# A seven-product SwiGLU kernel on one Trainium2 core: batch 0's val from unscaled tokens, 1/rms along rows by DMA, and all instruction orders redealt

## The chip, the cores and the metric

The kernel runs on one core of one Trainium2 chip. The metric is device microseconds of one execution. A profile of one execution stands beside the times. The engines are called PE (TensorE, matmuls), DVE (VectorE), ACT (ScalarE), POOL (GpSimd) and SP (SyncE, which issues most DMAs).

## The reference

`x` is (8, 8, 512, 64): batch, head, token, width. `state` is (8, 8, 32, 64). Attention goes both ways, and the tokens of all heads are then put side by side and sent through a feed-forward block:

```python
a = softmax(x @ state.T / 8);     xread = a @ state     # 512 tokens per batch
a2 = softmax(state @ x.T / 8);    sread = a2 @ x        # 32 tokens per batch
t = concat([xread, sread]) as (8 * 544, 512)
n = t / sqrt(mean(t * t, -1) + 1e-6) * rms_g
out = (silu(n @ w_gate) * (n @ w_val)) @ w_out          # 512 -> 1536 -> 512
```

The four weight arrays come as 64-bit floats and the kernel turns their bit patterns into 32-bit floats itself.

## The kernel before, in words

**Stages.** The tokens of one batch are one unit of work. Batch 0 is computed while the weights are still being loaded and converted. Batches 1 to 7 follow, each with the same sequence; while PE computes the products of batch b, the attention of batch b+1 is put in between. The 256 tokens of all states come last.

**Own weights.** Since `xread = a @ state`, the hidden products need not go over the 512 wide tokens: `own_weights` (L603) multiplies each batch's states by one pair of weight blocks ("pair mp", 256 columns of gate and of val; six pairs a batch; L616) and puts the result, v, into SBUF (L628). The hidden products are then of v with `aT_s`, the softmaxed scores (256 x 512 for a batch). `aT_s` is multiplied by 1/rms beforehand (L501), so gate and val both come out normalized.

**Weights at the start.** Eighteen pieces of 1 MB of raw bits (gate, val, out for each pair) are loaded, four ahead. ACT makes the exponents (`exponents`, L240, L243, L246), DVE the values (`values`, L267, L270, L276). Converted pairs are stored to DRAM and fetched again for each later batch (`fetch`, L189) into three buffers.

**Batch 0.** `scores` transposes x on PE (L334), ACT copies it (L336), PE multiplies it by the states (L361). `tokens_read` makes the softmax on DVE and ACT (L440 to L457), transposes it on PE (L465), and ACT copies it to `aT_s` (L468). The sum of squares goes over the Gram matrix of the states (L478, L481) and matmuls with a column of ones (`rms_on_array`, L392). `hidden` (L648) makes gate and val for one block of 128 hidden units (L659), silu (L665) and product (L669). The output projection goes on as blocks get ready (`project_as_ready`, L866) and is copied out by ACT (`projected`, L883).

**Batches 1 to 7.** `hidden_seven` (L753) makes the hidden products two blocks at a time by seven products in place of eight (L763), with sums on DVE (L826, L839, L845, L851). `project_twice` (L1035) does the output projection by seven outer products "o", each of seven inner ones (L1066), with sums of quarters and halves on DVE (L1114 to L1125) and of results on DVE (L1106) and POOL (L1092 to L1097). The weights' quarters for it are made once, on POOL, in batch 1 (`weight_quarters`, L1020), stored, and fetched.

**The read of tokens in a batch.** Within batch b, `tokens_read(b + 1)` runs: scores (L361), softmax, DVE transposes into `aT_s` (L460), a matmul that makes the tokens for their rms (L487), squares on ACT (L494), sums on DVE (L497). Then batch 1 uses `rms_on_array` (four matmuls with ones, L392), later batches `rms_on_blocks`: a matmul with `groups` (L415), the addition of 1e-6 (L420) and a power on POOL (`mean_root`, L293), which leaves 1/rms as 128 x 4. `along_rows` spreads that along the rows of all partitions by four transposes on PE (L300), and L501 multiplies `aT_s` by it. `slot_sums` (L681 to L684, POOL) makes the sums that the seven products need.

**States.** `states_read` makes the softmax of the other direction, the matmul with x (L557), a scaling on DVE (L568), a transpose on PE (L572). `state_norm` (L577) makes the rms of all 256 state tokens with eight matmuls by ones (L585).

**What sets the order.** Nothing is left to a scheduler. Each stage is a set of generators, one letter each, and strings say which generator takes its next step: `ORDER` for the start and batch 0, `FIRST` for batch 1, `PERIOD` for batches 2 to 6, `LAST` for batch 7, `STATES` for the end. The order of steps in the string is the order of instructions on every engine, and of the DMAs on the queue of the engine that issues them. `z` in `ORDER` is a matmul of the identity that keeps PE busy (`keep_awake`, L1198).

```python
for stream in FIRST if b == 1 else LAST if b + 1 == B else PERIOD:
    next(streams[stream])
```

The functions that the change touches:

Of the kernel before, what the change touches and what calls it, by code (L numbers as in the profile page):

```python
# [8 lines left out]
F32 = mybir.dt.float32  # L9
# [5 lines left out]
ALU = mybir.AluOpType  # L15
# [4 lines left out]
P = 128  # L20
RAW_AHEAD = 4
W_BUFS = 3
FLAT = 1793.0

ORDER = (
    "ddzzzzzzzzzezzzeezaaaaaaaaaaaaddaezddaseaaazzaeaaazzdaaaazdeezzzazzaaaazeeaaaadd"
    "aaadaaeAdadsdeezezAdavaaAvAAAAvhehteeAeAdddduhhppdAddtdeeedvvvudeeedphhdtheeddtA"
    "ddddeupdAAAdhAdedeeuedppvpsdAvvddAedhhpetudeeeddhtsAAdhudpAeppdddeAAeedddvAdsvvA"
    "eedphhtuseessseedddeeAhtsdhesppsdvdupdvvdhheeAddAdAtsshtpAudApAedpdhededdveuAApA"
    "AAvvheAdAtSAASSeSSdphSddShAtASuShAkuSSwwpwwkcpSScpSkkckpkcwkkkkkwwwwk"  # L30
)

PERIOD = (
    "vlhhatthhtaxxhvuxuthhthuhtauuhhtuhuhuthtahtuaaahuhhtuhuhuxhxtutxhthukkkhtaakavfx"
    "xxvgahuhuthuuuxhthhuuxtahtaaaaahuaxhuthhtuhhthhthhsppusuuuuffutaauuhpsspuppppukp"
    "ukkkkckkaakkgppkkcpppakooskakakakkppppacpppappppcckpfppcakakapppaakkkasskkgkaagg"
    "pppppppppppaakakkooakgapssskaaakkkoosspppcfpaawwsslpssxxxpcoowxxxfg"
)

FIRST = (  # L40
    "vhththhhthfhhuuuhtttuqqqqaxxaaauhthhhvquuhuxqxxaavtuhhththhfaxthhhqqquuuuxxtuhut"
    "hthhthhuaakaavfuuxhtuuhutthqqfhhutxxuqqqqqqhauthuuxhhaautthaaasshtuuhuuthuGhskuk"
    "GuGukkppqqpppqpppugqqpkkkklkppqpppkcpcqgaakppgqqkskaakaaaaqqppkkpppkppkkpkpkpkpa"
    "cosaaaacgpapgaskkkkkkaosaapppppgcppppcaappaskkakkapppkpapkappaakpookkoosaassfsww"
    "xssswxlscxxcoxofxg"
)
LAST = (
    "vxhhffththhtuhhhavuttuuhhtfuhhgxxthhhuuuxxtuthuhtthuhuxhutuvxxxvhthhutkxghhtuhut"
    "kxxhuukhtuhthhthhhhhuuuuttuthhhuuuuhtuhuutuupphuukkppcpapkkkkkpppppppppppkkkpcpp"
    "ckkppkckpkkpkpckkkpppkkkpkoppkpppagcpppppfkpkkkkkkkkppaaaapkpggppppacpcggooooooo"  # L50
    "a"
)
STATES = (
    "hththtyyhuhuhhttuhhhyyytyuhutuhhhutthtuyyhhuuyhhthhhuyututyyyhhtyuhhthuuuhhuhtth"
    "ythuuuyyyutuhuhuytuuyhthhuuhthtuhuhutuuppkhpuucppkkccpkpkpc"
)
# [3 lines left out]
def kernel(  # L60
# [62 lines left out]

    def load_state(b):

        rows[b] = two.tile([P, 2, D], F32, name="rows")
        for j in range(4):
            src = state[b, 2 * j:2 * j + 2].rearrange("e n d -> n e d")
            nc.sync.dma_start(out=rows[b][Ns * j:Ns * j + Ns], in_=src)

# [35 lines left out]
    x_d = [scratch.tile([4, 4, Ns, 4 * P], F32, name="x_d%d" % k) for k in range(2)]  # L166
    e_d = [scratch.tile([4, Ns, 4, 8 * Ns], F32, name="e_d%d" % k) for k in range(2)]
    w_sb = {}
    wo = consts.tile([P, NM, DM], F32, name="wo")
# [4 lines left out]
    for mp in range(NM // 2):  # L174
        for dram in (moe_w_gate, moe_w_val):
            pieces.append(dram[:, 2 * P * mp:2 * P * mp + 2 * P].rearrange("(i p) f -> p i f", p=P))
        pieces.append(
            moe_w_out[2 * P * mp:2 * P * mp + 2 * P].rearrange("(m p) f -> p m f", p=P))
# [12 lines left out]
    def home(k):  # L191

        mp, kind = divmod(k, 3)
        if kind == 2:
            return wo[:, 2 * mp:2 * mp + 2].rearrange("p m (i f) -> p m i f", f=P)
        return (w_sb[mp] if kind else new_w(mp))[:, :, :, kind, :]

# [108 lines left out]
    def scores(b, packed, soft):  # L306
# [22 lines left out]
        if b < 2:  # L329
            xT = one.tile([P, 4, NC, P], F32, name="xT", tag="xT")  # L330
            for c in range(NC):
                tp = aps.tile([P, 4, P], F32, name="at")
                for j in range(4):
                    TE.transpose(out=tp[:, j, :], in_=xb[:, c, P * j:P * j + P], identity=ident)  # L334
                yield
                SE.copy(xT[:, :, c, :], tp)  # L336
                yield "step"
# [48 lines left out]
    def rms_on_array(b, sq):  # L386

        sp = aps.tile([P, NC], F32, name="at") if b else fy.tile([P, NC], F32, name="f")
        order = (0,) if b else (0, 1)
        for i in order:  # L390
            for c in range(NC):
                TE.matmul(out=sp[:, c:c + 1], lhsT=sq[:, i, P * c:P * c + P], rhs=ones,  # L392
                          start=(c == 0 and i == order[0]),
                          stop=(i == order[-1]), skip_group_check=True)
        yield
        ss = two.tile([P, NC], F32, name="ss")
        VE.tensor_scalar(ss, sp, 1e-6, None, op0=ALU.add)
        yield "step"
        ri = mean_root(ss, NC)
        yield  # L400
        rp = along_rows(ri, NC) if b else along_rows(ri, NC, vps, "pv")
        yield
        return rp

    def rms_on_blocks(b, sq):
# [18 lines left out]
        yield  # L424
        rp = along_rows(ri, NC)
        yield
        return rp

    def tokens_read(b):
# [21 lines left out]
        for e in range(2):  # L451
# [15 lines left out]
            yield  # L467
            SE.copy(aT_s[b][:, e], tp.rearrange("p c t -> p (c t)"))  # L468
            yield "step"
# [13 lines left out]
        else:  # L483
# [12 lines left out]
            for i, j in ((0, 1), (2, 3), (0, 2)):  # L496
                VE.tensor_tensor(out=sq[:, i, :], in0=sq[:, i, :], in1=sq[:, j, :], op=ALU.add)  # L497
                yield
        rp = yield from (rms_on_array if b < 2 else rms_on_blocks)(b, sq)
        for e in (slice(0, 2),) if b else (slice(0, 1), slice(1, 2)):  # L500
            VE.tensor_tensor(out=aT_s[b][:, e], in0=aT_s[b][:, e],  # L501
                             in1=rp.unsqueeze(1).to_broadcast([P, e.stop - e.start, S]), op=ALU.mult)
        yield "step"
# [73 lines left out]
    def state_norm():  # L577

        sq = one.tile([P, NI, NT], F32, name="sqT", tag="eS")
        SE.activation(out=sq, in_=xsT, func=ACTF.Square, scale=DM ** -0.5)  # L580
        yield
        sp = aps.tile([P, NT // P], F32, name="at")
        for r in range(NT // P):
            for i in range(NI):
                TE.matmul(out=sp[:, r:r + 1], lhsT=sq[:, i, P * r:P * r + P], rhs=ones,  # L585
                          start=(i == 0), stop=(i == NI - 1))
        yield
# [15 lines left out]
    def own_weights(b, mp):  # L603
# [4 lines left out]
        def products():  # L608
            w = w_sb.pop(b * (NM // 2) + mp)
            for e in range(2):  # L610
                pv.append(vps.tile([P, 4 * P], F32, name="pv") if b and mp % 2 == 0 else
                          aps.tile([P, 4 * P], F32, name="at") if b or mp else
                          fx.tile([P, 4 * P], F32, name="f"))
            for j in range(4):
                for e in range(2):
                    TE.matmul(out=pv[e][Ns * j:Ns * j + Ns, :],  # L616
                              lhsT=stT_g[b][D * e:D * e + D, j, :],
                              rhs=w[D * e:D * e + D, j].rearrange("p m k f -> p (m k f)"),
                              start=True, stop=True)
            if b == 0 or b == 1 and mp < 2:  # L620
                fetch(b * (NM // 2) + mp + W_BUFS)
            yield

        def copies():
            v = (seven["v"] if b else v_0).tile([P, 2, 2, 2, P], F32, name="v")
            v_sb[b, mp] = v, None
            for e in range(2):
                SE.copy(v[:, e].rearrange("p m k f -> p (m k f)"), pv[e])  # L628
                yield
# [3 lines left out]

        return products(), copies()

    def more_of_v(b, mp):
# [10 lines left out]

    def hidden(m, lhs, rhs):  # L648


        gp, vp = [], []
        t = []
        h = hb[:, m, :]

        def products():
            for k, to in enumerate((gp, vp)):
                to.append(vps.tile([P, S], F32, name="pv"))
                for i, r in enumerate(rhs):
                    TE.matmul(out=to[0], lhsT=lhs(i, k), rhs=r,  # L659
                              start=(i == 0), stop=(i == len(rhs) - 1))  # L660
                yield

        def silu():
            t.append(two.tile([P, S], F32, name="t", tag="g"))
            SE.activation(out=t[0], in_=gp[0], func=ACTF.Silu)  # L665
            yield

        def gated():
            VE.tensor_tensor(out=h, in0=t[0], in1=vp[0], op=ALU.mult)  # L669
            yield  # L670

        return products(), silu(), gated()

# [205 lines left out]
    def projected(banks, store):  # L879
        spare = seven["s"].rearrange("p (r k) f -> p r (k f)", r=3)  # L880
        for r in range(4):
            ot = spare[:, r] if r < 3 else two.tile([P, DM], F32, name="ot", tag="g")
            SE.copy(ot, banks[r])  # L883
            store(r, 0, DM, ot)
            yield
# [298 lines left out]

    def of_batch_0(part):

        for m in range(NM):
            if m not in parts_0:
                parts_0[m] = hidden(m, lambda e, k, m=m: v_sb[0, m // 2][0][:, e, m % 2, k, :],
                                    [aT_s[0][:, e, :] for e in range(2)])  # L1190
            yield from parts_0[m][part]

    def keep_awake():
# [20 lines left out]

    parts_0, banks_0 = {}, []
    halves = load_parts(0)
# [7 lines left out]
    for k in range(2, RAW_AHEAD):  # L1224
# [4 lines left out]
               "e": exponents(), "d": values(),  # L1229
               "v": (step for mp in range(NM // 2) for part in own_weights(0, mp) for step in part),  # L1230
               "h": of_batch_0(0), "t": of_batch_0(1), "u": of_batch_0(2),
               "p": project_as_ready(banks_0), "c": projected(banks_0, store_tokens(0)),
# [69 lines left out]
```

## Time and profile before

| what | us |
|---|---|
| time, median of 3 runs (lowest, highest) | 758.01 (757.89, 759.5) |
| profiled execution: span from first to last instruction | 756.2 |
| one steady batch (381.05 to 461.21, first product to first product) | 80.2 |
| batch 1 (133.15 to 220.72) | 87.6 |
| first hidden product of batch 0 (L659) starts at | 32.46 |
| last matmul ends about | 752.8 |

The page of the profile gives the profiled execution's span but no time of its own; the median of the runs is 1.8 above the span, and that is what lies around it. Busy time is the time in which an engine has an instruction under way. The chain that ended last is followed backward from the last instruction: at each step to what released it, or to the instruction before it on the same engine. The waits list how long an engine stood for another one's result. The slices of the whole span, each 18.9 us, show PE near full from the second one on:

```profile
PE   8999999999899999999999999999999999999998
```

### The profile page before, as it was taken

What the parts mean: (1) busy time and instruction counts of PE and PEld (TensorE: products, weight loads), DVE (VectorE), ACT (ScalarE), POOL (GpSimd) and SP (SyncE); (2) the same over time, 40 slices, a digit from 0 to 9 for tenths busy, and PEclk for the clock granted to TensorE, in tenths of its full rate; (3) what the DMA queues carried; (4) which work ended last, traced back from release to release, by engine and by line L of the source; (5) the groups of instructions that cost most, each with busy time, mean ns of one, the idle gap of its engine ahead of it and who ended that gap; (6) DMA issues with size and microseconds to landing.
All of it is one profiled execution on the core that took longest, in us unless ns stands there. A gap on an engine that the chain in (4) does not pass through costs nothing.

```text
span 756.2 us, 14360 instructions
## 1 busy us (share of the span) xinstructions
PE 743.2 (98%) x5618; PEld 592.0 (78%) x5618; DVE 578.7 (77%) x979; ACT 351.7 (47%) x546; POOL 294.2 (39%) x380
## 2 busy tenths in 40 slices
PE   8999999999899999999999999999999999999998
PEld 6534444778768898879877997799788987899997
DVE  3887776679957996689947994799579965787961
ACT  5998965553235523643255425543456236411220
POOL 2000003892584326532474129312842275323600
PEclk9999999999999999999999999999999999999999
DMA  9986954695576176725684377517661865132311
GB/s 281 281 299 227 314 211 151 248 294 163 201 228 240 32 291 209 281 56 198 243 284 112 135 274 253 175 69 299 215 225 27 305 204 218 51 98 114 140 56 29
DMA packets 61891, 146.17 MB, mean 193 GB/s; under 512 B 15744, under 2 KB 32640, under 8 KB 54912
## 3 DMA queue, kind: packets, MB, share of 16 engines
q1 hardware_dynamic: 48704, 125.78, 47.8%
q10 hardware_dynamic: 13120, 19.47, 8.9%
q8 instruction: 45, 0.74, 0.4%
q14 instruction: 22, 0.18, 0.1%
HBM read 116.46 MB, written 28.77 MB: 192 GB/s over the span
## 4 chain that ended last, share of the span: by engine, by line
PE 91%; DVE 5%; ACT 3%; issue 1%; POOL 0%; DVEq 0%; POOLq 0%
PE f L763 38%; PE f L1066 28%; PE pv L659 5%; PE f L866 5%; PE at L616 3%; PE pv L616 3%; PE f L929 2%; PE f L1198 2%; PE at L557 1%; PE at L361 1%; PE at L487 1%; DVE hb L1125 0%; PE at L300 0%; ACT ex L243 0%; PE at L334 0%
## 5 line engine op out<-in xcount | busy, mean ns | idle before, releaser
L763 PE MATMUL f<-aT_s,v 128*128 128x256 f32 x504 | 119.6, 382 | 0.0
L763 PEld LDWEIGHTS f<-aT_s,v 128*128 128x128 f32 x504 | 94.5, 190 | 24.8 <-issue 8.4
L1092 POOL TENSOR_TENSOR kept<-kept 128x256 f32<-128x256 f32 x28 | 23.1, 824 | 174.9 <-DVE kept L1106 173.8
L826 DVE TENSOR_TENSOR g<-g,f 128x512 f32<-128x512 f32 x84 | 57.4, 686 | 40.0 <-PE f L763 35.9
L1076 ACT COPY kept<-f 128x512 f32<-128x512 f32 (+1 forms) x56 | 29.6, 532 | 123.9 <-PE f L1066 82.2
L763 PE MATMUL f<-aT_t,vs 128*128 128x256 f32 x336 | 87.1, 383 | 0.0
L1066 PE MATMUL f<-w,h 128*128 128x128 f32 x588 | 74.6, 276 | 0.9 <-DVE h L1116 0.8
L763 PEld LDWEIGHTS f<-aT_t,vs 128*128 128x128 f32 x336 | 62.5, 190 | 15.4 <-POOL vs L643 4.2
L1066 PEld LDWEIGHTS f<-w,h 128*128 128x128 f32 x588 | 69.6, 192 | 5.3 <-issue 4.1
L817 ACT ACTIVATE hb<-g 128x1024 f32<-128x1024 f32 x42 | 44.4, 1058 | 56.9 <-DVE g L826 56.8
L643 POOL TENSOR_TENSOR vs<-v 128x256 f32<-128x256 f32 x42 | 31.4, 748 | 79.5 <-ACT v L628 79.5
L293 POOL TENSOR_TENSOR ri<-ss,mhalf 128x4 f32<-128x4 f32 x8 | 10.7, 1341 | 116.7 <-DMA w_m<-w_d 84.1
L815 ACT COPY g<-f 128x512 f32<-128x512 f32 x42 | 24.6, 586 | 45.0 <-PE f L763 45.0
L763 PE MATMUL f<-aT_t,v 128*128 128x256 f32 x168 | 43.5, 381 | 1.6 <-DVE c L826 1.6
L866 PE MATMUL f<-wo,hb 128*128 128x512 f32 x96 | 44.8, 603 | 0.0
L659 PE MATMUL pv<-aT_s,v 128*128 128x512 f32 x96 | 43.9, 595 | 0.0
L763 PE MATMUL f<-aT_s,vs 128*128 128x256 f32 x168 | 43.6, 382 | 0.0
L839 DVE TENSOR_TENSOR hb<-hb,c 128x512 f32<-128x512 f32 (+1 forms) x48 | 36.6, 763 | 7.9 <-ACT hb L817 7.2
L839 DVE TENSOR_TENSOR hb<-hb,f 128x512 f32<-128x512 f32 (+1 forms) x48 | 31.0, 646 | 15.1 <-PE f L763 15.1
L1066 PE MATMUL f<-wo,h 128*128 128x128 f32 x336 | 42.2, 275 | 0.0
L1066 PE MATMUL f<-wo,hb 128*128 128x128 f32 x336 | 42.1, 275 | 0.0
L826 DVE TENSOR_TENSOR c<-c,f 128x512 f32<-128x512 f32 (+1 forms) x48 | 31.2, 651 | 12.6 <-PE f L763 12.6
(204 smaller groups left out, 1657.7 us busy)
## 6 DMA issues: line engine op xcount, KB each, us to landing
w_m<-w_d SPq DMA_DIRECT2D x48, 1024.0 KB, 5.8
w<-t_d SPq DMA_DIRECT2D x49, 576.0 KB, 5.1
out_dram<-kept SPq DMA_DIRECT2D x56, 128.0 KB, 1.9
raw<-in_moe_w_val_dram SPq DMA_DIRECT2D x6, 1024.0 KB, 5.4
raw<-in_moe_w_out_dram SPq DMA_DIRECT2D x6, 1024.0 KB, 8.5
w_d<-w_m SPq DMA_DIRECT2D x6, 1024.0 KB, 4.9
x_b<-in_x_dram SPq DMA_DIRECT2D x6, 1024.0 KB, 7.7
x_d<-xB ACTq DMA_DIRECT2D x6, 1024.0 KB, 4.2
```

Of the source, the lines that this page charges most:

```text
L616: TE.matmul(out=pv[e][Ns * j:Ns * j + Ns, :], lhsT=stT_g[b][D * e:D * e + D, j, :], rhs=w[D * e:D * e + D, j].rearrange("p m k f -> p (m k ...
L643: GE.tensor_tensor(out=vs[:, 0], in0=a21, in1=a22, op=ALU.add)
L659: TE.matmul(out=to[0], lhsT=lhs(i, k), rhs=r, start=(i == 0), stop=(i == len(rhs) - 1))
L763: TE.matmul(out=ps[:, i, 0:half], lhsT=l[:, i, :], rhs=r, start=(start and i == 0 and k == 0), stop=(k == len(lhs) - 1), skip_group_check= ...
L815: SE.copy(gates(q)[1], q["x"][:, :, 0:half])
L817: SE.activation(out=hb[:, 2 * mp:2 * mp + 2, 0:n].rearrange("p m (c t) -> p m c t", c=2), in_=q["g"][:, :, :, 0:half], func=ACTF.Silu if s ...
L826: VE.tensor_tensor(out=to, in0=to, in1=q[ps][:, :, 0:half], op=ALU.add)
L839: VE.tensor_tensor(out=part, in0=part, in1=val, op=ALU.mult)
L866: TE.matmul(out=banks[r], lhsT=hb[:, m, P * r:P * r + P], rhs=wo[:, m, :], start=(m == 0), stop=(m == NM - 1))
L1066: TE.matmul(out=to[half][:, slot, :], lhsT=lhs[:, k, :], rhs=rhs[:, k, :], start=(fresh and n in (0, 4) and k == 0), stop=(k == QM - 1), s ...
L1076: SE.copy(k[:, 4 * i:4 * i + 4 - i], banks[name][i])
L1092: GE.tensor_tensor(out=k[:, 1:3], in0=k[:, 0:1].to_broadcast([P, 2, QD]), in1=k[:, 1:3], op=ALU.add)
```

## The change

- **Orders.** All five strings are dealt anew.
- **Pieces.** The val piece of a pair is loaded and converted ahead of its gate piece.
- **Batch 0, tokens.** `aT_s` is kept unscaled. The row of 1/rms is copied to SBUF (`row`) and a scaled copy `aT_n` is made. Val products use `aT_s`. Gate products use `aT_s` for the first two blocks, whose result is multiplied by `row`, and `aT_n` for the rest. Since val is left without its 1/rms, `projected` multiplies each row of tokens by it (a column of `ri`).
- **Batch 0, pair 0.** `first_own_weights` makes val's half and then gate's half of the own weights.
- **Copies.** Copies of xT alternate between ACT and DVE; one of batch 0's two `aT_s` copies, and one of each two v copies, goes to DVE.
- **1/rms along rows.** From batch 1 on, `rms_on_blocks` is used, and 1/rms goes to DRAM and comes back broadcast to all partitions, by two DMAs on SP, in place of the four transposes.
- **Banks.** For batches 2 to 7, the own weights of pair 1 go to the banks `fy` and `fz`.
- **state_norm.** The four squares are added on DVE, and two matmuls with ones are left of eight.

The strings apart, the core of the diff is:

```diff
-        for dram in (moe_w_gate, moe_w_val):
+        for dram in (moe_w_val, moe_w_gate):
...
-                SE.copy(xT[:, :, c, :], tp)
+                (VE.tensor_copy if c % 2 else SE.copy)(xT[:, :, c, :], tp)
...
         ri = mean_root(ss, NC)
         yield
-        rp = along_rows(ri, NC)
-        yield
-        return rp
+        nc.sync.dma_start(out=r_d[b % 2].rearrange("c p -> p c"), in_=ri)
+        yield
+        nc.sync.dma_start(out=sq[:, 2, :], in_=r_d[b % 2].rearrange("c p -> (c p)")
+                          .unsqueeze(0).to_broadcast([P, S]))
+        yield
+        return sq[:, 2, :]
...
-            SE.copy(aT_s[b][:, e], tp.rearrange("p c t -> p (c t)"))
+            (VE.tensor_copy if e else SE.copy)(aT_s[b][:, e], tp.rearrange("p c t -> p (c t)"))
...
-        rp = yield from (rms_on_array if b < 2 else rms_on_blocks)(b, sq)
+        rp = yield from (rms_on_blocks if b else rms_on_array)(b, sq)
+        to = aT_s[b]
+        if b == 0:
+            row = rms_0["row"] = x_0.tile([P, S], F32, name="row")
+            SE.copy(row, rp)
+            rp = row
+            yield
+            to = x_0.tile([P, 2, S], F32, name="aT_n")
+            aT_n.append(to)
+        VE.tensor_tensor(out=to, in0=aT_s[b], in1=rp.unsqueeze(1).to_broadcast([P, 2, S]),
+                         op=ALU.mult)
...
+        for n in (NI // 2, NI // 4):
+            VE.tensor_tensor(out=sq[:, 0:n], in0=sq[:, 0:n], in1=sq[:, n:2 * n], op=ALU.add)
+            yield
         sp = aps.tile([P, NT // P], F32, name="at")
         for r in range(NT // P):
-            for i in range(NI):
-                TE.matmul(out=sp[:, r:r + 1], lhsT=sq[:, i, P * r:P * r + P], rhs=ones,
-                          start=(i == 0), stop=(i == NI - 1))
+            TE.matmul(out=sp[:, r:r + 1], lhsT=sq[:, 0, P * r:P * r + P], rhs=ones,
+                      start=True, stop=True)
...
+    def first_own_weights():
+        w = w_sb[0]
+        v = v_0.tile([P, 2, 2, 2, P], F32, name="v")
+        v_sb[0, 0] = v, None
+        for k in (1, 0):
+            pv = [fx.tile([P, 2, P], F32, name="f") for e in range(2)]
+            for j in range(4):
+                for e in range(2):
+                    TE.matmul(out=pv[e][Ns * j:Ns * j + Ns],
+                              lhsT=stT_g[0][D * e:D * e + D, j, :],
+                              rhs=w[D * e:D * e + D, j, :, k, :], start=True, stop=True)
...
+            for e in range(2):
+                (VE.tensor_copy if e else SE.copy)(v[:, e, :, k, :], pv[e])
+                yield
...
+        def product(pool, name, m, k, tokens):
+            ps = pool.tile([P, S], F32, name=name)
+            for e in range(2):
+                TE.matmul(out=ps, lhsT=v_sb[0, m // 2][0][:, e, m % 2, k, :], rhs=tokens[:, e],
+                          start=(e == 0), stop=(e == 1))
+            return ps
...
+            for m in range(2):
+                v[m] = product(vps, "pv", m, 1, aT_s[0])
+                yield
+            for m in range(2):
+                g[m] = product(fx, "f", m, 0, aT_s[0])
+                yield
+            for m in range(2, NM):
+                g[m] = product(vps, "pv", m, 0, aT_n[0])
+                yield
+                v[m] = product(vps, "pv", m, 1, aT_s[0])
+                yield
...
+            for m in range(2):
+                VE.tensor_tensor(out=new_t(m), in0=g[m], in1=rms_0["row"], op=ALU.mult)
+                yield
...
-            SE.copy(ot, banks[r])
+            SE.mul(ot, banks[r], rms_0["column"][:, r:r + 1])
```

## The prediction, made before the changed kernel was run

> **What bounds the kernel.** I read the clock first, then busy time, then the chain that ended last, then a table by stage, then what TensorE (PE) waits for. The granted clock is 1.00 all through, so no step is about it.
>
> ```profile
> PE 743.2 (98%) x5618; PEld 592.0 (78%) x5618; DVE 578.7 (77%) x979; ACT 351.7 (47%) x546; POOL 294.2 (39%) x380
> PE 91%; DVE 5%; ACT 3%; issue 1%; POOL 0%; DVEq 0%; POOLq 0%
> ```
>
> PE is busy nearly always and is 91% of the chain: what PE does is what the span costs, so an instruction taken from PE is paid out in full where PE waits for nobody. Where it does wait shows by stage (columns: window, then PE, PEld, DVE, ACT, POOL busy with counts, clock, DMA share, GB/s):
>
> ```profile
> 133.00:221.00 88.00, 83.75 (x672) 68.52 (x665) 72.01 (x118) 33.57 (x58) 60.74 (x66) 1.00 0.68 222
> 381.00:461.00 80.00, 80.00 (x670) 68.19 (x662) 64.57 (x115) 34.97 (x59) 34.73 (x45) 1.00 0.59 199
> ```
>
> The lower row is a steady batch (batches 2 to 6): PE is busy 80.00 of 80.00. The upper row is batch 1, which runs from 133.15 to 220.72, 87.6 against 80.2 for a steady one (381.05 to 461.21). In the first batch-1 window PE waits for VectorE (DVE):
>
> ```profile
> PE f L763 <- DVE c L826: 1.6, 1, 1.6
> PE at L487 <- DVE aT_s L460: 1.0, 1, 1.0
> PE f L1066 <- DVE h L1116: 0.8, 1, 0.8
> PE at L572 <- DVE sr L568: 0.7, 1, 0.7
> ```
>
> So three places have something to win or lose: PE's own work everywhere, the start, and batch 1; and the steady batch, which has no wait, can only get one. These are the rows I price with (start, duration, engine, line, tile):
>
> ```profile
> 452.28 0.13 PE at L415 x2
> 455.19 0.44 PE at L300 x4
> 664.91 1.68 PE at L585 x16
> 423.83 0.68 DVE L839 TENSOR_TENSOR hb<-hb,f 128x512 f32<-128x512 f32 x1
> 441.57 0.70 DVE L460 STREAM_TRANSPOSE aT_s<-eS 128x512 f32<-128x512 f32 x1
> 442.93 0.66 PE L487 MATMUL at<-aT_s,rows 32*64 32x512 f32 x4
> 453.20 1.39 POOL L293 TENSOR_TENSOR ri<-ss,mhalf 128x4 f32<-128x4 f32 x1 [1.54 <-DVE ss L420]
> out_dram<-kept SPq DMA_DIRECT2D x56, 128.0 KB, 1.9
> rms_g<-in_moe_rms_g_dram SPq DMA_DIRECT2D x1, 2.0 KB, 7.2
> ```
>
> **1. PE work that goes: -4.9.** The four transposes that spread 1/rms along rows (L300) take 0.44 in the chain. They go in batches 1 to 7: 28 transposes at 0.44 / 4 = 0.11, 3.1. Batch 1's sum of squares goes from four ones-matmuls (0.81, from 112.81 to 113.62) to the groups matmul of the later batches (0.13): 0.7, and I take 0.6. state_norm's eight ones-matmuls (1.68 for 16 records) become two: 1.68 x 6/8 = 1.26. Sum 4.9. It is on the path because PE is; the two DVE adds that replace the six matmuls (0.69 and about 0.4) lie beside PE's projection, and the pow and the spread behind them have at most 0.5 of PE wait to give, which I put into the end's bounds.
>
> **2. The start: +0.8.** Batch 0's first hidden product starts at 32.46, and before it PE mostly waits. The change wants the val product earlier, from tokens not yet scaled. By the new order of instructions it does not get it. (a) Seventeen keep-awake matmuls stand ahead of the first transpose instead of thirteen; 4 are 8 records at 0.21, 1.7, so the step at 9.33 comes at about 11.0. (b) ACT's second xT copy now stands behind two exponent steps of 0.73; the scores matmul, at 13.36, comes at about 15.2. (c) From about 17.1 DVE has its instructions back to back up to the copy of v: reading the old rows for each, some 16 us, to 33.1. The work it got there (two xT copies 1.1, one aT_s copy 0.6, v's copy 0.35, small ones 0.5) is more than what left it (L501, 1.28). With one more xT copy (0.55) and the scaling of the state read (0.45) the first val product comes at 34.5, 2.0 later. (d) But by then PE has done more of what it must do anyway: e transposes 0.86, the state read 1.03, one chunk of x 0.43, and 0.43 of row transposes stand later; 1.9 in all. Net 0.1. (e) Then pair 1's own weights wait about 0.5 and the first gated block about 0.25 for conversions on DVE (43.5 against 42.95): +0.75. Pair 2 is converted at 58.1 for a need at 58.65, pair 3 at 71.8 for 76.9, so nothing is added there. Bounds: if DVE's queue does not hold, the tokens are ready at 25.2 and PE starts at about 27, -5.4; if (d) is wholly lost to waits, +2.5.
>
> Where the new gate work hides: in batch 0 m = 0 and 1 need one more DVE multiply each (0.69), m from 2 on read the scaled copy. The last copies (L883) become a multiply by a column on ACT; I take the 0.6 of ACT's other copies of 128x512 for it, and ACT is busy 47%.
>
> **3. Batch 1: -4.5.** Its excess is 7.4. DVE is busy 72.0 against 64.6, since its operations are stretched while GpSimd does the weight quarters (L1020): L845 takes 1.37 at 161.61, 0.68 in a steady batch. In the new order 23 of the 28 quarter steps stand ahead of the first projection step (17 before), the tokens of batch 2 arrive at its scores some 27.4 us into the batch instead of 33.4, and the DVE work that PE waited for after the hidden part is done before it. One wait stays: the read of tokens (now L490) stands after three of the seven outer products instead of four, and DVE is no faster there. I leave 2.5 to 3 of the 7.4. Bounds: all of it goes, -7.4; none, 0.
>
> **4. Steady batches: 5 x 0.8 = +4.0.** This is what the DMA costs in place of the transposes, by way of the order. To make time for a trip to DRAM and back, the read of tokens moves from 442.93 to where, in the old trace, PE stands at 437.5. It needs DVE's second aT_s transpose, which ends at 441.57 + 0.70 = 442.27, 0.66 ahead of its reader. In the new order I count the DVE instructions from the last gate product (L839 at 423.83) to that transpose: 13.8 to 14.5 us by their old rows, so it ends at 437.9 to 438.5. PE then waits 0.4 to 1.0, and about 0.2 more for the quarter sum behind it. I take 0.8. Bounds: 0 if DVE is only 0.5 faster than I count; 1.3 each, 6.5, if the projection's sums wait as well.
>
> The DMA itself: two transfers in a row, ri (128x4) to r_d as 512 separate elements, and r_d back, broadcast to 128 partitions of 2 KB. They were not in the old kernel. The groups matmul stands 13.2 us ahead of the next batch's first product in the new order; ri is ready 2.9 later (DVE 0.33 and 0.67, pow 1.39, hand-overs), and L511's multiply takes 1.22, so **the pair may take 9.0 us** at no cost. The nearest rows: a 128 KB store lands in 1.9, twice that is 3.8; rms_g, the same 512 elements of 4 bytes, took 7.2 amid the first loads, twice that is 14.4. The return is 256 KB in long runs, nearer to the store, and the write is to DRAM with far fewer bytes than rms_g's neighbours in the queue; I take 6, hidden. SP issues both and stands at each until its data is there; behind them wait one store of 128 KB and the fetch of pair 3's weights (below). Behind the multiply (L511) on DVE wait the two scalings of the state read, and for those PE's transpose of it. The Trainium skill, "DMA: Bandwidth & Descriptors", Rules for kernel authors, speaks against this form: a strided last dimension becomes one descriptor per element, and the data should be laid out contiguously instead. Its section Anatomy of one DMA gives about 2.0 us fixed plus bytes over 436 GB/s, by which the pair would be an estimated 4.6; by that too it stays hidden, and only rms_g's row says otherwise. Batch 1's pair has 24.7 us.
>
> **5. Pair 3's weights: 6 x 0.2 = +1.2.** The next batch's own weights of pair 3 move up from 465.84, 4.6 after its first product, to right behind that product. Their 1 MB goes into the buffer that pair 0 gives back, so it can be issued only when PE is through with pair 0. From there PE has, by the rows of the chain, 1.02 (pair 1), 1.03 (state read), 0.67, 0.13, 0.67, 0.13, 0.86 and 1.02 (pair 2), 5.5. In the old trace these loads landed in 5.1 at the least and 5.5 in the median of three. So PE waits between nothing and 0.6; I take 0.2, for batches 2 to 7.
>
> **6. End: 0, bounds -0.5 and +0.5.** The last batch and the states are redealt, but after the last matmul (752.8) there is 3.4 of copy and store either way, and only 0.5 of wait for hb ahead of it.
>
> **Sum.** -4.9 + 0.8 - 4.5 + 4.0 + 1.2 = -3.4. From the span of 756.2 that gives 752.8. Runs have a median of 758.0, 1.8 more than the profiled span, which I add: **754.6**.
>
> **Rivals.**
> A. The start is won: if DVE reaches the first val product's inputs by 29 instead of 33, then 3.5 to 5.4 are saved there instead of 0.8 lost, and the time is about 749.5. For it: the tokens are needed without the scaling. Against it: L501's 1.28 is all that this takes from DVE ahead of it.
> B. Slower: **the DMA pair is late.** PE's first product of a batch waits for L511, and all behind it. It decides from 9.0 us a pair; in the six batches with that room, at 9.6 the gain is gone (3.4 / 6). With 11.0, from between the two rows, it is 6 x 2.0 = 12 and the time 767; with 14.4 it is 32. For it: rms_g's 7.2. Against it: the 1.9 row, and 24.7 us in batch 1.
> C. DVE is late at the read of tokens by 1.3 in every batch, and batch 1 gains only 2.5 to 4.5 for the same reason: -4.9 + 0.8 + 6.5 + 1.2 less that is -0.9 to +1.1, 757 to 759, and 760.5 with the weights 0.5 late. For it: that transpose has 0.66 to spare now and is asked 5 us sooner. Against it: the old order puts 5 us of quarter sums ahead of it that can stand behind.
> D. The change does not do what it says: val from unscaled tokens begins no sooner than before. That is already in my start term, and giving it up wholly changes nothing more.
>
> **Chances.** Forecast 0.60 (750.5 to 756.5, its own range from the bounds of batch 1 and the steady batches), A 0.09, C 0.19, B 0.12. "Same" is within 0.2%, 756.5 to 759.5, about what a measurement here can tell. Faster: the forecast and A, 0.69. C gives 0.13 same and 0.06 slower; with B slower is 0.18. Range 749 to 760.5: it leaves out B and the far end of A, some 0.15 to 0.2.
>
> **What would show it.** The first val product near 34.5 (A: by 29). In steady batches no along-rows transposes, one wait of PE on aT_s of 0.4 to 1.0 at the read, one on the weights of pair 3 of 0 to 0.6, and a period of 80.2 - 0.44 + 1.0 = 80.8 (C: 81.3 and more). The r_d transfers landing within 9.0 together; if L511 is what the first product waits for, B. Batch 1 near 83. What would make me wrong: a DMA pair above 9.0, DVE's count before the read, or DVE's queue in the start being shorter than I add up.

## The result

The changed kernel takes 845.5 us (median of 4 runs, 841.7 to 845.8) against 758.1 for the kernel before: a ratio of 1.113 (95% interval 1.110 to 1.116). The profiled execution, the fastest of the four, has a span of 839.9, 83.7 more than before. The forecast was 754.6, in a range of 749 to 760.5.

In the page of the changed kernel, busy time, granted clock and the chain show at once that it is bound by something else:

```profile
PE 756.0 (90%) x5588; PEld 602.2 (72%) x5588; DVE 581.2 (69%) x999; ACT 362.6 (43%) x549; POOL 283.1 (34%) x380
...
PEclk9999999899999987999699997999799997999999
...
PE 59%; DMA 17%; DVE 16%; POOL 3%; issue 2%; ACT 2%; ACTq 1%; DVEq 0%; POOLq 0%
```

PE's share of the chain is 59% instead of 91%, DMAs have 17% where they had none, and PE's clock is no longer full everywhere. What PE waits for (first lines of the waits; total, times, longest):

```profile
PE at L567 <- DMA e<-e_d: 63.3, 6, 12.9
PE f L1123 <- DMA w<-t_d: 3.7, 1, 3.7
```

L567 is the read of states (L557 before). Its e, the softmax numbers of the other direction, goes to DRAM and back (e_d) to be turned round. The issues of DMAs, before and after (KB each, median us to landing):

```profile
e_d<-eB ACTq DMA_DIRECT2D x6, 512.0 KB, 3.0
e<-e_d ACTq DMA_DIRECT2D x24, 128.0 KB, 3.2
```

```profile
e_d<-eB ACTq DMA_DIRECT2D x6, 512.0 KB, 9.3
e<-e_d ACTq DMA_DIRECT2D x24, 128.0 KB, 7.2
sq<-r_d SPq DMA_DIRECT2D x7, 256.0 KB, 4.6
...
r_d<-ri SPq DMA_DIRECT2D x7, 2.0 KB, 10.1
```

Nothing was changed about e's transfers themselves. One steady batch in time shows who stands beside them: the instructions before the change, those after it, and then PE, clock and DMA after it by stretches of 8 us (columns as in the prediction). DVE turns e, ACT issues the store and the loads, PE reads:

```profile
443.57 1.24 DVE L539 STREAM_TRANSPOSE eB<-e 128x1024 f32<-128x1024 f32 x1
444.84 0.35 ACTq L542 DMA_DIRECT2D e_d<-eB  x1
447.94 2.05 ACTq L546 DMA_DIRECT2D e<-e_d  x4
456.57 1.10 PE L557 MATMUL at<-x_b,e 128*32 128x64 f32 x64
```

```profile
298.62 0.38 SPq L425 DMA_DIRECT2D r_d<-ri  x1
299.63 1.23 DVE L549 STREAM_TRANSPOSE eB<-e 128x1024 f32<-128x1024 f32 x1
300.90 0.35 ACTq L552 DMA_DIRECT2D e_d<-eB  x1
308.51 0.33 SPq L427 DMA_DIRECT2D sq<-r_d  x1
310.28 2.65 ACTq L556 DMA_DIRECT2D e<-e_d  x4
313.21 1.22 DVE L511 TENSOR_TENSOR aT_s<-aT_s,sq 128x1024 f32<-128x1024 f32 x1 [9.37 <-DMA sq<-r_d]
319.24 1.07 PE L567 MATMUL at<-x_b,e 128*32 128x64 f32 x30 [12.14 <-DMA e<-e_d]
```

```profile
300.00:308.00 8.00, 7.10 (x79) 5.52 (x78) 3.84 (x6) 0.00 (x0) 4.42 (x7) 1.00 0.72 66
308.00:316.00 8.00, 0.00 (x0) 0.00 (x0) 1.47 (x3) 2.05 (x4) 1.34 (x2) 0.61 0.79 214
316.00:324.00 8.00, 4.76 (x79) 4.62 (x80) 0.77 (x3) 0.03 (x1) 4.97 (x8) 0.53 0.88 290
```

The 2 KB of 1/rms are issued at 298.62. From 300 to 308 all queues together move 66 GB/s. e's store is issued at 300.90, ACT issues the loads at 310.28, when it has landed, and they end at 319; PE has stood still for 12 us by then, and works at half its clock behind that.

Where the 83.7 come from, by the first hidden product of each batch:

| stretch | before | after | difference |
|---|---|---|---|
| up to batch 1 | 133.1 | 131.5 | -1.5 |
| batch 1 | 87.6 | 97.4 | +9.8 |
| batches 2 to 6 | 400.9 | 477.5 | +76.6 (15.3 each) |
| batch 7 and states | 134.6 | 133.5 | -1.2 |

### The profile page after: what moved, and what is told of

It is laid out like the page before. It is cut to its first block, busy times and chain, and to the rows that moved or that the text cites. A ratio compares the mean times of both kernels' runs of the same rounds, so it can differ in the third digit from the quotient of the medians.

```text
span 839.9 us, 14333 instructions
## 1 busy us (share of the span) xinstructions
PE 756.0 (90%) x5588; PEld 602.2 (72%) x5588; DVE 581.2 (69%) x999; ACT 362.6 (43%) x549; POOL 283.1 (34%) x380
## 4 chain that ended last, share of the span: by engine, by line
PE 59%; DMA 17%; DVE 16%; POOL 3%; issue 2%; ACT 2%; ACTq 1%; DVEq 0%; POOLq 0%
PE f L820 29%; PE f L1123 12%; DMA e_d<-eB 7%; DMA e<-e_d 5%; PE pv L693 4%; PE f L923 4%; PE f L986 2%; PE at L628 2%; DVE h L1171 1%; PE pv L628 1%; DMA xG<-x_d 1%; DVE sq L500 1%; PE at L567 1%; DVE kept L1163 1%; DMA w<-t_d 1%
## 5 line engine op out<-in xcount | busy, mean ns | idle before, releaser
L1149 POOL TENSOR_TENSOR kept<-kept 128x256 f32<-128x256 f32 x28 | 20.8, 743 | 166.4 <-DVE kept L1163 155.9
L641 ACT COPY v<-pv 128x512 f32<-128x512 f32 x42 | 22.7, 589 | 114.2 <-issue 97.5
L567 PE MATMUL at<-x_b,e 128*32 128x64 f32 x512 | 13.0, 278 | 63.3 <-DMA e<-e_d 63.3
L567 PEld LDWEIGHTS at<-x_b,e 128*32 128x32 f32 x512 | 11.4, 148 | 69.5 <-issue 43.0
L677 POOL TENSOR_TENSOR vs<-v 128x256 f32<-128x256 f32 x42 | 33.5, 798 | 80.5 <-ACT v L641 80.5
L511 DVE TENSOR_TENSOR aT_s<-aT_s,sq 128x1024 f32<-128x1024 f32 x7 | 8.6, 1225 | 61.5 <-DMA sq<-r_d 61.5
L896 DVE TENSOR_TENSOR hb<-hb,c 128x512 f32<-128x512 f32 (+1 forms) x48 | 33.1, 690 | 13.0 <-ACT hb L874 12.2
```

Source lines behind the costliest of these rows:

```text
L567: TE.matmul(out=rp[Ns * j:Ns * j + Ns, e, :], lhsT=(e2T[:, j, e, c, :] if b > 1 else flat[:, e, c, Ns * j:Ns * j + Ns]), rhs=(xb[:, h, c, ...
L641: (SE.copy if b or not e else VE.tensor_copy)(v[:, e].rearrange("p m k f -> p (m k f)"), pv[e])
L677: GE.tensor_tensor(out=vs[:, 0], in0=a21, in1=a22, op=ALU.add)
L896: VE.tensor_tensor(out=part, in0=part, in1=val, op=ALU.mult)
```

## The experiments

Theory 1: the write of 512 single elements holds up the DMAs around it. Rival 2: the new order has e's store too near its reader (in the traces DVE starts to turn e 13.0 us ahead of the read before the change; after it 7.5 ahead of 307.1, when PE is ready for the read). Rival 3: SP stands at the return and lets a burst go.

**Take the trip away.** rows_on_PE spreads 1/rms by PE again:

```diff
-        nc.sync.dma_start(out=r_d[b % 2].rearrange("c p -> p c"), in_=ri)
         yield
-        nc.sync.dma_start(out=sq[:, 2, :], in_=r_d[b % 2]...to_broadcast([P, S]))
-        yield
-        return sq[:, 2, :]
+        rp = along_rows(ri, NC)
+        yield
+        return rp
```

> The changed kernel with 1/rms spread by four transposes on PE again in all batches, and no trip through DRAM; everything else, the orders too, as changed. Theory 1 (the write of 512 single elements holds the DMA engines, and the store and loads of e behind it come late): the store of e lands in 3 to 3.5 us (9.3 with the write), PE's wait at the read of states falls from 12 to at most 2.5 a batch, the time to 755 to 768. Rival 2 (the new order has the store of e 7.5 us ahead of its reader where it was 13.1, and that is what PE waits for): the wait stays at 8 or more, the time above 815.

Measured: 768.3, ratio 1.014 (1.009 to 1.019). e's store lands in 2.7, and PE waits 4.8 for e in all, at most 1.3 at once:

```profile
e_d<-eB ACTq DMA_DIRECT2D x6, 512.0 KB, 2.7
```

```profile
PE at L565 <- DMA e<-e_d: 4.8, 6, 1.3
```

The time is at the upper end of theory 1's range, and far below rival 2's.

> As rows_on_PE, but 1/rms is still written to DRAM element by element and nobody reads it. Theory 1: the write alone does the harm, PE waits 10 to 12 us a batch and the time is 830 to 846. Rival 3 (SP stands at the return transfer for 9 us and then lets stores and fetches go in a burst, against which e's loads compete; or the multiply is late): without the return nothing stands on SP, and the time is that of rows_on_PE within 8 us.

Measured: 824.8, ratio 1.087 (1.083 to 1.090). e's store lands in 9.5, PE waits 48.2 for it in five batches. The write does most of it; rival 3 (the return, and what stands behind it) accounts for at most the 20.7 between this and 845.5. The lower bound of theory 1's range was missed by 5.

**Other forms of the same 2 KB.** write_16_bytes and flipped_rows:

```diff
+        nc.sync.dma_start(out=r_d[b % 2].rearrange("c p -> (c p)").rearrange("(p c) -> p c", c=NC), in_=ri)
```

```diff
-        TE.matmul(out=sp, lhsT=groups.rearrange("p i t -> p (i t)"), rhs=part, ...
+        TE.matmul(out=sp, lhsT=part, rhs=groups[:, 0, :], start=True, stop=True)
...
+        nc.sync.dma_start(out=r_d[b % 2].rearrange("c (g t) -> (c g) t", t=Ns), in_=ri)
```

> The changed kernel with the same 2 KB written as 128 runs of 16 bytes, each partition's four numbers side by side, instead of 512 of 4 bytes; so every token gets another token's 1/rms. Theory 1, by count of runs: the write lands in about 3 to 4 us instead of 10.1, the store of e in 4 or less, the time is 755 to 775. If the price hangs on the bytes or on the round trip itself, the write still takes about 10 and the time stays above 835.

> The changed kernel with the groups matmul turned round (part as weights, groups as the moving side), so that the sums of squares lie as 16 rows of 32 tokens, and 1/rms is written as 16 runs of 128 bytes. The power on GpSimd then has 16 partitions of 32 numbers instead of 128 of 4. Theory 1: the write lands in about 2 us, the store of e in 3 to 4, time 755 to 768; more by what the power takes above 1.4 us, if the multiply then ends behind the first product's turn. If the trip through DRAM is what costs, above 835.

Measured: 779.7 (1.027, 1.024 to 1.030) and 779.1 (1.028, 1.024 to 1.031), with the writes landing in 3.4 and 1.3. The store of e lands in 2.9 in both, as theory 1 said, but both times came out above its ranges. In flipped_rows the power takes 5.67 on 16x32 numbers, 1.39 on 128x4, so the write and the return come later, and PE waits 12.8 for e's loads, which run beside the return; that the return delays them was not tried. In write_16_bytes PE waits 20.6 for e's loads, which took up to 9.0, at the same time as a fetch of weights and three stores that SP lets go behind the return.

**Mend the order instead.** e_early only moves letters "s" of PERIOD (places from 0): the two exponentials from 236 and 241 to behind 153 and 157, the turning and the store of e from 253 and 254 to behind 213, its four loads from 255, 256, 257 and 261 to behind 235. rows_on_PE_e_early and 16_bytes_e_early have the same string.

> The changed kernel with the element-by-element write kept, and only the order of batches 2 to 6 edited: the state softmax's exponentials, the transpose and store of e, and its loads are issued earlier, ahead of the write of 1/rms. Theory 1 (the write slows what is in the DMA engines with it): the store of e lands in 3 us again and PE does not wait for e; what is left late is the multiply by 1/rms, since write and return take 14.7 us of the 9.0 they may, 2.5 to 5.7 a batch: 770 to 800. If PE still waits 8 or more for e, the write's harm does not hang on what is in flight with it: above 825.

> As rows_on_PE (four transposes, no trip through DRAM) with the order of e_early. In rows_on_PE each steady batch was 2.5 us longer than in the kernel before, and PE waited 0.8 to 1.3 of it for e. If the late store of e is the rest of the loss, that wait goes and the time is 757 to 764; if the order is late for other reasons (x of the scores, weights of pair 3, DVE), it stays at 766 or more.

> The write in 128 runs of 16 bytes with the order of e_early; the multiply reads the returned row in the permuted order, so each token gets its own 1/rms. Theory 1: no wait for e, write and return in 7 of the 9.0 us, PE's transposes saved: 755 to 765. If the weights and stores behind the return still hold up e's loads, 768 to 780.

Measured: 822.7 (1.083, 1.077 to 1.090), 801.9 (1.054, 1.050 to 1.058), 797.4 (1.052, 1.045 to 1.059): all three missed, in part by a mistake in the edit. The longest wait of PE, and a wait of ACT, in 16_bytes_e_early:

```profile
PE f L1128 <- ACT kept L1138: 14.0, 5, 5.2
```

```profile
ACT kept L1138 <- DMA e<-e_d: 35.6, 4, 10.7
```

The loads are issued by ACT, and ACT stands at the first until the store has landed. Put ahead of ACT's copies of the projection, they make PE wait for those. In e_early, which keeps the element-by-element write, that is 16.0 of PE's waits; it waits 0.4 for e, but 8.0 for a result of DVE (L578) and 5.9 for weights besides, so the mistake is not all that keeps it slow. In rows_on_PE_e_split the loads stay where they were, and turning and store go behind 212 and 218:

> As rows_on_PE_e_early, but the loads of e stay where rows_on_PE has them, behind ACT's copies of the projection, and the store of e is issued after the squares; in rows_on_PE_e_early ACT stood at the loads for up to 11 us and PE waited for its copies. If that was all that went wrong there, and the late store of e was PE's wait in rows_on_PE: 758 to 766. If it stays at 768, e is not what the order of rows_on_PE loses by.

Measured: 773.7 (1.020, 1.017 to 1.022). PE no longer waits for e, but 3.6 for weights, 2.1 at the groups matmul and 1.3 for x. So taking away the wait for e does not win the loss back, and no single instruction was found that does.

**Is it the clock?** filled_wait puts 54 matmuls of the identity ahead of the read of states:

```diff
+        for _ in range(54 if b > 1 else 0):
+            TE.matmul(out=rp.rearrange("p e d -> p (e d)"), lhsT=ident, rhs=ident, start=True, stop=True)
```

> The changed kernel with 54 extra 128x128 matmuls of the identity (0.223 us each, 12.0) ahead of the read of states in batches 2 to 7, into a tile that is overwritten; they fill PE's wait and change no result. If the granted clock falls to 0.5 to 0.7 because PE stood idle, it stays at 1.00 and each period loses the 2.6 us of stretched matmuls: 825 to 833. If the clock falls for another reason, or the stretch is not the clock's, the time stays at 842 to 850.

Measured: 846.7 (1.115, 1.112 to 1.118), so the time forecast failed, though the clock is 1.00 in every steady batch. Batches 2 to 6 take 94.0 each instead of 95.5, although the gap (12.3 of matmuls and 1.4 of wait in the batch from 334.5) is 1.2 longer than the wait it replaces: some 2.7 a batch for the clock. Over the five batches that gains 7.5. Batch 1, where there was little to fill, pays 8.4 for the matmuls, and in this execution the start is 3.4 longer, with a clock of one half for 6.8 us from 31.5; together that more than cancels it.

**The write in the old kernel.** before_plus_write adds one line to the kernel before, behind the power; nobody reads the result. before_plus_early_write instead writes 512 numbers of a constant, ahead of e's store. The added line of the first:

```diff
         ri = mean_root(ss, NC)
+        nc.sync.dma_start(out=r_d[b % 2].rearrange("c p -> p c"), in_=ri)
```

> The kernel before, with one thing added in the read of tokens of batches 2 to 7: 1/rms is also written to DRAM as 512 single elements when it is ready, and nobody reads it. There the loads of e have landed by then (453.2 against 454.6). Theory 1 (the write harms what is in the DMA engines with it, and PE only if that is urgent): the write takes about 10 us, e lands as before, the time is 757 to 765. If the write costs a batch 10 us or more wherever it stands, above 810.

> As before_plus_write, but the 512 elements are those of a constant and are issued after the squares, some 5 us ahead of the store of e. Theory 1: the store of e lands in 6 us or more instead of 3.0, its loads come 3 to 6 us later, and since they had 3.4 to spare PE waits 0 to 3 a batch: 758 to 775. If the store of e keeps its 3 us, theory 1 is wrong on how the harm is done.

Measured: 802.4 (1.056, 1.053 to 1.060) and 800.8 (1.055, 1.053 to 1.057). The second does to e what was said (its store lands in 8.3), but costs far more than was said. The first refutes the milder part of theory 1: with e long landed, the six writes still cost (800.1 - 756.2) / 6 = 7.3 each on the mean. The cost is uneven: from first product to first product the stretches from batch 1 to batch 6 are 0.1, 18.4, 0, 8.0, 11.5 and 0 longer, and what follows 6.1. PE's waits there, and 12 us of one batch, in which the write is issued at 302.80:

```profile
PE f L765 <- ACT g L812: 16.5, 4, 5.9
PE at L574 <- DVE sr L570: 12.5, 3, 7.1
```

```profile
304.00:308.00 4.00, 2.71 (x86) 1.69 (x70) 1.06 (x1) 1.07 (x2) 3.77 (x7) 1.00 0.31 75
308.00:312.00 4.00, 0.00 (x0) 0.00 (x0) 0.00 (x0) 0.00 (x0) 3.92 (x6) 0.62 0.02 4
312.00:316.00 4.00, 2.21 (x15) 1.69 (x23) 0.77 (x3) 0.45 (x1) 0.05 (x1) 0.50 0.75 244
```

For 4 us the 16 DMA engines move 4 GB/s, with 1 MB of weights issued. What PE waits for then is whatever needed a transfer next: a store of results whose tile ACT wants back (ACT waits 20.1 in all for these stores), or DVE, which stands for 8.1 with no engine to wait for. Behind four of the six writes one packet of the instruction queues took 2.99 to 3.27 us, and no other packet of them took more than 1.43 in this run; that DVE waits for its instructions is possible, but was not tried.

**What of the write does it?** Four more forms in the same place; for the last, r_d has 128 numbers for every one that is written:

| run | runs of bytes | in DRAM | lands in | time | ratio (interval) |
|---|---|---|---|---|---|
| before_plus_write | 512 of 4 | side by side | not waited for (10.1 in the changed kernel) | 802.4 | 1.056 (1.053 to 1.060) |
| write_128_of_4 | 128 of 4 | side by side | 9.1 | 780.8 | 1.029 (1.024 to 1.034) |
| before_plus_write_16 | 128 of 16 | side by side | 2.0 | 759.3 | 1.001 (0.999 to 1.002) |
| write_512_of_16 | 512 of 16 | side by side | 5.0 | 759.7 | 1.002 (1.000 to 1.003) |
| write_512_spread | 512 of 4 | 512 bytes apart | 2.3 | 760.2 | 1.001 (1.000 to 1.003) |

```diff
-        nc.sync.dma_start(out=r_d[b % 2].rearrange("c p -> p c"), in_=ri)
+        nc.sync.dma_start(out=r_d[b % 2].rearrange("c p f -> p c f")[:, :, 0], in_=ri)
```

> As before_plus_write, with the unread 2 KB written as 128 runs of 16 bytes. The 512-element write cost 43 us there for six writes, 7.2 each, though e had landed: behind it hardly any packet of any queue moved for 8 us. By the count of runs, a quarter: a standstill of about 2 and 0 to 2 a write, 759 to 771. If the price is one of a write of less than 512 bytes a run as such, whatever their number, 790 or more.

> As before_plus_write, but only one column of 1/rms is written: 128 single elements of 4 bytes in a row of DRAM. before_plus_write (512 of 4 bytes) cost 43 us, before_plus_write_16 (128 of 16 bytes) nothing that can be told. By the count of runs alone: 759 to 761, like 128 of 16 bytes. If what is slow is many 4-byte runs falling into the same few hundred bytes of DRAM, a quarter of 43 is lost: 766 to 772.

> As before_plus_write, with 512 runs of 16 bytes (8 KB of other numbers, four runs from each partition, to places 2 KB apart). By count of runs: as with 512 of 4 bytes, 795 or more. By their size or by how many fall side by side in DRAM: 760 to 775.

> As before_plus_write, 512 single elements of 4 bytes, but each goes to a place of its own 512 bytes from the next in DRAM. By count of runs or by their being short: 795 or more. If the standstill comes from neighbours (each 4-byte write waiting for the one before it in the same piece of DRAM), it goes: 759 to 768.

The same 512 elements of 4 bytes, spread, cost nothing that can be told from no change (1.6 us between the medians) instead of 43. The stretches behind that write, issued at 294.3, in its trace:

```profile
296.00:300.00 4.00, 4.00 (x109) 2.97 (x109) 1.32 (x4) 1.55 (x3) 3.84 (x7) 1.00 0.42 98
300.00:304.00 4.00, 4.00 (x36) 2.68 (x16) 0.29 (x1) 2.35 (x5) 3.84 (x7) 1.00 1.00 384
```

So neither the count nor the shortness alone makes the standstill, but 4-byte writes lying side by side. 128 of them cost half of what 512 do, not a quarter, and land hardly sooner (9.1, against 10.1 for 512 in the changed kernel). Why neighbours do it, and how far apart is enough between 4 and 512 bytes, was not tried. Theory 1 is right that the write is the cause and wrong on what about it.

**Where did the forecast gain go?** old_period keeps the change's start, batch 1, last batch and states, takes PE's transposes for 1/rms, and the old PERIOD string and banks for batches 2 to 6.

> The changed kernel's start, batch 1, last batch and states, with the transposes on PE for 1/rms, and for batches 2 to 6 the order and the banks of the kernel before. From the pieces measured so far: start 0.9 sooner, batch 1 3.0 shorter, steady batches 80.2 as before, end 0.7 shorter; 4.6 less than before, a time of 752 to 756. If the gain of the start and of batch 1 is given back where the orders meet, 757 to 760.

> old_period with six more keep-awake matmuls in the start: three behind the eight (18.1 to 21.7), two ahead of the second transpose of states, one between the first two chunks of x. In old_period's profile the granted clock is 0.5 for 6.8 us from 31.3 on, and its first product of batch 1 comes at 135.8 where runs of the same start without that stretch have 131.2 to 132.3. If this is what eats the gain of the start, the time is 1.5 to 3.5 below old_period's 758.0; if the six matmuls (0.43 each) only delay PE, 758 to 760.

> As old_period_awake, with the order of the last batch of the kernel before too (its two added DVE additions share a step with the matmuls). In old_period PE waited 2.3 for weights once, and its last batch took 76.7 where the kernel before takes 74.7. If that wait comes from the two orders meeting, 1 to 2 less than old_period_awake, 753 to 756; if not, the same as that.

Measured: 757.95 (0.9989, 0.9978 to 1.0001), 757.4 (0.9977, 0.9962 to 0.9993), 759.5 (1.0012, 0.9996 to 1.0029). Steady batches are 80.2 again. In old_period the clock is at 0.83 on the mean from 20 to 40:

```profile
20.00:40.00 20.00, 17.58 (x178) 11.69 (x177) 17.51 (x34) 15.75 (x23) 1.94 (x1) 0.83 0.78 216
```

```profile
20.00:40.00 20.00, 19.43 (x209) 12.45 (x209) 19.17 (x36) 17.29 (x25) 1.94 (x1) 1.00 0.83 250
```

The second row is old_period_awake's: with six matmuls more the clock stays, and its first product of batch 1 comes at 132.9 instead of 135.8. The mean clocks of all runs say the same: five of old_period's twelve have 0.995 or less, none of old_period_awake's eleven is below 0.998. It is the one version whose interval lies below the kernel before, by 0.23%. It is 0.6 below old_period, not the 1.5 to 3.5 expected, and as the two intervals overlap the times alone do not show a difference. Of the 4.6 expected for old_period, the profile of old_period_awake has 2.8 (span 753.4), its median 1.0. The old order of the last batch removed its wait of 1.6 for weights, but the states' part then took 61.8 instead of 59.3, so it was no gain. No run shows a form of the trip through DRAM that pays: with the changed orders its best is 779.1, against 768.3 with the transposes (rows_on_PE).

## Why the prediction was wrong, step by step

**Step 4, the DMA pair: this is what failed.** "I take 6, hidden" against 10.1 + 4.6 = 14.7. The upper end, 14.4 from rms_g's row, comes close, but by luck: it is a load's 7.2 taken twice, where the write took 10.1 and the return 4.6. I chose the lower end because the write has fewer bytes around it. The 4.6 of the Trainium skill's fit ("DMA: Bandwidth & Descriptors", Anatomy of one DMA) was too low as well; the page gives that fit for DMAs issued from GpSimd, and these are issued by SP.

**What the pair's lateness costs: wrong in kind.** I priced it, in rival B, as the multiply by 1/rms coming late, 32 us with 14.4. In the trace the multiply ends at 314.4, 4.8 before the read of states begins; it is not what PE waits for. The lateness that I priced was there, but hidden behind the longer wait: without that, an estimate from the same rows has PE at the first product at about 311.7 (319.24 - 12.14 + 4.6 from the read to the product), 2.7 ahead of the multiply's end. The price was paid by the other transfers: of the 76.6 in batches 2 to 6, 62.9 go when the trip through DRAM goes (414.6 in rows_on_PE), 12.6 a batch, nearly all of it PE's wait for e and the clock behind it (some 2.7). No row of the trace of before showed such a write, and an earlier load of 512 elements says nothing of what a store does to others; the range, which assumed that a late transfer is late for its own reader alone, could not hold it.

**A move that I did not count.** The turning, store and loads of e are put behind the groups matmul, 5.5 us nearer to their reader. Without the write PE waits 0.4 to 1.3 a batch for e; with it, it put e's store inside the standstill.

**Step 4, the read of tokens: wrong mechanism.** The waits list none of PE on aT_s there, neither in the changed kernel nor in rows_on_PE; the count of DVE was near the mark, since in rows_on_PE the reader's first matmul starts at 360.05, the second transpose ends at 360.27 and the next matmul starts at 360.33, held up by 0.3 at most. The order does cost, 13.7 in rows_on_PE where I had 4.0 + 1.0 for these batches, but by waits for e (4.4) and weights (2.1); the scores' matmuls, which read x, are busy for 1.8 to 2.1 a batch in three of these batches instead of 1.1 to 1.2, and the rest was not taken apart. **Step 5** (weights of pair 3, 0.2, bound 0.6): PE waits 1.8 and 0.3 for weights in two batches of rows_on_PE and not in the others.

**Step 6 held, step 1 is only partly shown.** The end is 1.2 shorter, of which I had 1.26 from state_norm. The transposes are gone from batches 1 to 7, but every run without them loses more elsewhere, so no run shows the 3.1 that I had for them.

**Step 2, the start, held in its rows:** first transpose at 11.16 (forecast 11.0), scores at 15.45 (15.2), first val product at 34.92 (34.5). Batch 1 begins 0.9 to 1.5 sooner (131.5 in the changed kernel and 132.2 in rows_on_PE, against 133.1), where my terms for that stretch give about 0.2 sooner; part of it may be chance, since with the start of the kernel before it begins between 132.4 and 134.0. What I missed is that fewer matmuls keep PE awake later in the start, and that in some executions the clock halves there from about 31 for 6.8 us.

**Step 3, batch 1:** 3.0 shorter in rows_on_PE, forecast 4.5; in the changed kernel 9.8 longer, and two of the seven pairs are behind that. I gave batch 1's own pair 24.7 us. It is issued at 109.0, ahead of batch 1, and POOL, whose order is fixed, starts the sums of aT_s at 125.41 instead of 119.09 in rows_on_PE; behind them its other sums are late, PE waits 2.6 for these at 148.7 and 1.5 for ACT at 153.4, and the clock falls to half for 6.8 us. That is rival B's mechanism, by way of POOL. The next write, at 210.08, stands inside the batch: PE waits 3.7 for weights and 1.7 for e.

The Trainium skill's rule against a strided last dimension ("DMA: Bandwidth & Descriptors", Rules for kernel authors) spoke against this form, and I gave that 0.12; here the measured cost bears it out for 4-byte elements side by side, while in the kernel before elements 512 bytes apart and runs of 16 bytes cost 0.2% or less by the medians (1.001 and 1.002).

## What to carry to other kernels

Before a small transfer is put into a full pipeline, ask what it does to the transfers beside it, not only when it lands; where no row shows such a transfer, try it unread in the old kernel, which here needed one line. Here single 4-byte elements side by side in DRAM cost all queues, while in the kernel before runs of 16 bytes, or elements 512 bytes apart, did not; other sizes and spacings would have to be tried. And an issue that waits for another transfer belongs on a queue whose engine has nothing urgent behind it.

## What the runs showed of the hardware

- 512 elements of 4 bytes side by side in DRAM: nearly all their packets start and end between 299 and 301 in the batch shown; then from 303 to 309 only 36 other packets end, where 121 and 191 end in the us from 298 and from 299, and one that starts at 302 takes 5.2 us.
- The clock fell to one half in stretches of 3.4, 6.8, 10.2 or 13.7 us (13.7 behind most waits of 12 us in the changed kernel), and stayed full in the steady batches when the wait was filled. "TensorE: Matmul & The Clock Gate" of the Trainium skill (The HAM clock gate) says that it halves after an idle window of about 3.4 us; for the long waits these traces agree. It also halved around shorter ones: at 149.4 in the changed kernel, next to waits of 2.6 and 1.5, and at 387.8 in rows_on_PE_e_split, next to one of 2.2; and in the start with PE at 88% busy by the profile, in some executions only.
- The power on GpSimd does not go by the count of numbers in all: with 512 each time it took 1.39 us as 128x4 and 5.67 as 16x32.
